# Batches 0 and 1 of a banded attention in blocks of 58 queries, v by single heads on ACT's queue, and a newly searched order

## The chip, the cores and the metric

The kernel runs on one core of one Trainium2 chip. The metric is the device time of one execution in microseconds, lower is better. The core has TensorE (PE, with its weight loads shown as PEld), VectorE (DVE), ScalarE (ACT), GpSimd (POOL) and SyncE (SP). SP, ACT and POOL also issue DMA transfers, each on a queue of its own.

## What is computed

Attention on 8 batches of 8 heads, 576 tokens, head size 64. Each head has two parts that are added: softmax attention between means of four tokens (144 pooled positions), repeated four times, and softmax attention in a band of plus or minus three tokens. Then a two-layer feed-forward with the ELU.

```python
q_d, k_d, v_d = (t.reshape(B, H, S // 4, 4, D).mean(axis=3) for t in (q, k, v))
out_up = np.repeat(sm_attn(q_d, k_d, v_d), 4, axis=2)     # softmax(q k^T / 8) v
mask = np.abs(pos[:, None] - pos[None, :]) < 4
out_local = masked_softmax(q @ k.T / 8, mask) @ v
x = (out_up + out_local).transpose(0, 2, 1, 3).reshape(4608, 512)
h = x @ w_in                                              # 512 x 2048
g = np.where(h > 0, h, np.exp(np.minimum(h, 0)) - 1)
return g @ w_out                                          # 2048 x 512
```

## The kernel before

The work is cut into named operations, each on one engine. A planner (`Plan`, a list scheduler with a rank and an assumed duration for each operation) simulates the engines while the program is built, and the operations are then written out in the order that it found. That order is fixed: each engine runs its own list in order, and waits at an operation until what it reads is there. The ranks come from the table `PARAM`, with corrections for single operations in `FIRST`. Some parameters choose the engine (`e_...`), some gate a weight load behind a cast (`G0` to `G8`, by `WGATE`) or the loads of batch 1 behind an event of batch 0 (`L0` to `L4`, by `LGATE`; a small memset on DVE holds the load back).

Heads go in pairs, j = 0 to 3 for each batch b. For a pair the operations are, by name: `load{b}{j}q` and `k` (SP, some of the k by POOL with a cast on the way), `cast{b}{j}0` and `1` to fp16, `tq` and `tk` (PE: transposes and sums of four tokens at once, L645, L648, L662), `evq` and `evk` (evictions from PSUM by ACT or DVE, L685, L686), `sc` (scores, L757), `ex` (one exponential on ACT over both parts, L787), `mask` (DVE, L792; for batch 0 the mask is instead added by PE, L763), `den` (PE sums the exponentials, L810), `recip` (DVE, L828), `spr` (PE spreads the reciprocals over the partitions, L841), `evr` (its eviction, L850), `out` (L883), `xn` (DVE normalizes, L910, L914), `add` (the pooled part is added, L933, into `xt`, blocks of 512 tokens).

v is loaded for all heads of a batch at once (`vm{b}0`, `vm{b}0h`, `vm{b}2`, `vm{b}2h`; two lots of four heads, two halves of keys), cast by `vc{b}{j}`, and pooled on PE by `tv` (L705, L722), evicted by `evv`. The local part cuts the 576 tokens into 6 blocks of 96. A block has two halves of 48 queries, each against 64 keys on 64 partitions, so that two halves and two heads fill the 128 by 128 array in four tiles of 64 by 64. Batches 0 and 1 (`SIX`) take a way of their own for q and k: their rows are loaded six tokens to a partition, in long pieces.

The feed-forward has nine blocks of 512 tokens: `mm1_{t}_{fc}` (L950, 4 matmuls of 512 columns), an exponential (ACT, L956), two operations on DVE (L958, L961), and `mm2_{t}_{tt}{part}` (L979, 4 matmuls), then `os` (ACT, L995) and the store. w_in comes in four chunks, w0 to w3 (`WI`), w_out in w4 to w7 (`WO`), all on POOL's queue, with a cast. Attention of batch b+1 is interleaved with the feed-forward of block b. Before the first mm1 there is only batch 0 and the first transposes of batch 1; where PE has nothing ready there, the planner writes matmuls on zeros (`fill`, L357).

All hardware transfers, those of SP and of ACT, share eight semaphores in turn, in the order in which the program lists them together: each transfer waits, on the engine that issues it, for the landing of the transfer eight before it.

Of the kernel before, what the change touches and what calls it, by code (L numbers as in the profile page):

```python
# [16 lines left out]
SD = S // 4  # L17
# [23 lines left out]
BY_PE = (0, 1)  # L41
WIC = (0, 512, 1024, 1536, 2048)
# [22 lines left out]
class Plan:  # L65
# [197 lines left out]
    def emit(self):  # L263
        for o in self.order:
# [8 lines left out]
PARAM = dict(e_d0=2, e_d1=0, e_d2=0, e_d3=1, M0=27.21, P=36.34, LAG=0.71, LEAD=52.25, GAP=6.32, SC=5.0,  # L273
             DEN=30.8, OUT=1.3, OUTG=2.09, LOAD=15.53, VLOAD=34.45, VCAST=9.57, warm=3.4, FILL=36.0, WI=-28.49,
             WO=59.77, WOG=5.01, OVER=1.64, LEAD1=58.97, GAP1=6.47, OUT1=55.0, VLOAD1=29.88, LOAD1=41.47,
             CC=-34.39, tv0=-22.07, C0=-2, SC0=3.1, OUTA=-23.54, OUTB=-20, DEN0=2.92, DENB=-27.58, SPA=-26.75,
             SPB=-20.86, V0=-43, G0=0, G1=0, G2=0, G3=2, G4=12, G5=6, G6=12, G7=3, G8=13, L0=0, L1=1, L2=2,
             L3=4, L4=4, LAG0=0.75, BY4=-51.82, TV1=0.68, C1=-19.87, e_cq0=0, e_cq1=1, e_cq2=1, e_cq3=1,
             e_ck0=0, e_ck1=0, e_ck2=1, e_ck3=1, e_q0=1, e_q1=0, e_q2=0, e_q3=0, e_k0=1, e_k1=1, e_k2=0,
             e_k3=0, QG=2.5, tvA=-26, e_v0=2, e_v1=1, e_v2=2, e_v3=1, e_g0=1, e_g1=1, e_g2=1, e_g3=1, e_r0=1,  # L280
             e_r1=0, e_r2=1, e_r3=1, e_xr0=0, e_xr1=1, e_xr2=0, e_xr3=1, e_a0=1, e_a1=0, e_a2=1, e_a3=0,
             e_xq0=1, e_xq1=0, e_xq2=1, e_xq3=0, e_xk0=1, e_xk1=0, e_xk2=1, e_xk3=1, KS=-64, KSG=3, e_s0=0,
             e_s1=1, e_s2=1, e_s3=0, e_xs0=0, e_xs1=1, e_xs2=1, e_w0=0, e_w1=1, e_w2=0, e_w3=0, e_xs3=0)

FIRST = {
    "add000": 0.72, "add001": 3.11, "add010": 0.8, "add011": 1.42, "add020": -0.47, "add030": 1.32,
    "add031": 0.68, "cast000": 0.77, "cast011": 1.41, "cast021": 4.15, "cast030": 0.71, "den00": -0.64,
    "den02": -0.88, "evk00": 0.17, "evk01": -0.98, "evk03": 0.21, "evq00": -5.46, "evq01": -5.01,
    "evq03": 0.38, "evr01": -3.98, "evr02": -2.25, "evv01": 6, "evv02": -2.4, "evv03": 0.21, "ex00": -5.19,
    "ex01": 5.05, "ex02": 0.83, "ex03": -1.67, "load00k": -4.99, "load01k": -2.41, "mask1": 6, "mask6": -3.11,  # L290
    "out00": -0.66, "out01": 4.25, "out02": -0.47, "out03": 1.13, "recip02": -2.47, "sc01": 0.78,
    "sc03": -0.22, "select": -0.15, "sixths": -1.87, "spr00": -2.79, "spr01": -3.25, "spr02": -1.4,
    "spr03": -1.43, "tens": 0.56, "tk00": -5.07, "tk01": -0.72, "tk02": 3.96, "tk03": 1.15, "tq00": 3.92,
    "tq01": 0.71, "tq02": -1.94, "tv00": -4.97, "vb": 1.68, "vc00": 2.37, "vc01": -3.26, "vc02": -4.17,
    "xn00": -1.03, "xn01": -5.03, "xn02": -0.06,
# [4 lines left out]
def kernel(  # L300
# [15 lines left out]
    def many(kind, shape, dt=FP16):  # L316
# [8 lines left out]
        "qt": many("qt", [128, 720]),  # L325
        "kt": many("kt", [128, S + 16]),
        "ex": many("ex", [128, 2, EW]),
        "vd": many("vd", [128, 3, NPAIR, 128]),
        "rcb": many("rcb", [128, NPAIR, 2, GW]),
        "rc": many("rc", [128, HD]),  # L330
        "xn": many("xn", [128, 2 * GW]),
# [32 lines left out]
    def const(name, shape):  # L364
        return sb.tile(shape, FP16, tag=name, name=name)
# [3 lines left out]
        "BY6": const("BY6", [QB, NB, SD]),  # L369
        "VR": const("VR", [128, 32]),  # L370
        "VB": const("VB", [128, 28]),
        "BND": const("BND", [128, KR + KB]),
        "MASK": const("MASK", [128, NB, KB]),
        "NEG": const("NEG", [128, NB, KB]),
        "FIRST": const("FIRST", [128, 32]),
        "PICK": const("PICK", [128, 2, 51]),
# [12 lines left out]
    def sixths():  # L389
        band(C["BY6"][:], [[1, NB], [-4, SD]], 6, 0, 3)  # L390

    def clears():
# [4 lines left out]
        nc.vector.memset(C["VB"][:], 0.25)  # L397
        nc.vector.memset(C["ONE"][:, QB:], 0.25)
# [5 lines left out]
    def marks():  # L404
# [5 lines left out]
        for i in range(4):  # L410
            nc.vector.memset(pick[32 * i : 32 * i + 24, 1, 19 + i // 2 : 20 + i // 2], 1.0)
        nc.vector.memset(first[:], 0.0)
# [27 lines left out]
    def mask1():  # L440
        band(C["BND"][:], [[-1, KR + KB]], 1, 0, 6)

    def mask6():
        m = C["MASK"]
        for h in range(2):
            one = C["BND"][KR * h : KR * h + KR, KR * h : KR * h + 1]
            nc.vector.tensor_copy(out=m[KR * h : KR * h + KR], in_=_free(one, [[0, NB], [1, KB]]))
        nc.vector.memset(m[0:3, 0], 0.0)

# [6 lines left out]
    def fours():  # L456
# [6 lines left out]
    c_m6 = op("DVE", 0.65, -57, mask6, after=[c_m1], name="mask6")  # L463
    c_mask = op("POOL", 0.25, -56, edge, after=[c_m6], name="edge")
    c_one = op("DVE", 0.2, PARAM["BY4"], eye_one, after=[c_eye], name="eye_one")
    c_neg = op("DVE", 0.6, -54, lambda: nc.vector.tensor_scalar(
        out=C["NEG"][:], in0=C["MASK"][:], scalar1=-1.0, scalar2=30000.0, op0=AB.add, op1=AB.mult), after=[c_mask], name="neg")
# [3 lines left out]
    c_vr = op("DVE", 0.35, -54, fours, after=[c_vb], name="fours")  # L471
# [74 lines left out]
    def load_v(b, parts=(0, 2)):  # L546
# [6 lines left out]

        def blocks(lo, hi, tok, n):
            return bass.AP(tensor=a.tensor, offset=a.offset + (lo * QB + tok) * D, ap=[[D, n], [QB * D, hi - lo], [1, D]])

        def main(c0, c1, h, eng):
            t = at(x32)[KR * h : KR * h + KR]
            if b == 0 and c0 == 0 and h == 0:
                nc.vector.memset(t[0:3, 0:1, :], 0.0)  # L560
                nc.sync.dma_start(out=t[3:KR, 0:1, :], in_=blocks(0, 1, 0, KR - 3))
                c0 = 1
# [6 lines left out]

# [526 lines left out]
```

## Time and profile before

| What | Value |
|---|---|
| Median of 3 runs | 349.24 us (347.39 to 349.95) |
| Profiled execution, its own time | 349.04 us |
| Its span, first to last instruction | 347.3 us |
| PE busy | 331.9 us, 96% |
| DVE, ACT, POOL busy | 218.0, 196.4, 132.6 us |
| Mean granted clock of TensorE | 0.984 |
| mm1 (L950), mm2 (L979) | 576 and 592 matmuls, 141.6 and 141.5 us |
| First mm1 starts at | 34.12 us |
| DMA moved | 49.73 MB, mean 143 GB/s |

Busy time of an engine overlaps that of the others. Busy times of single matmul groups overlap too, since matmuls are pipelined: 576 matmuls at a mean of 380 ns are 219 us of durations in 141.6 us of busy time. Gaps are what PE's timeline shows between groups, with what released it in brackets.

### The profile page before, as it was taken

The numbers are of one execution on the slowest core, as the hardware profiler recorded it, in microseconds if no ns is written. First come the engines' busy times: TensorE is split into PE (matmuls) and PEld (weight loads), VectorE is DVE, ScalarE is ACT, GpSimd is POOL, SyncE is SP. The second block draws the span as 40 slices with busy tenths as digits, with TensorE's granted clock in tenths as the row PEclk, the third lists the DMA queues.
The fourth block names the chain that finished last, engine by engine and source line by source line (L and its number), as shares of the span: only waits on it lengthen the run. The fifth ranks groups of instructions, "written<-read, shape, count | busy, mean of one in ns | idle before, by whom it ended". The sixth has DMA issues, their size and how long they took to land.

```text
span 347.3 us, 10965 instructions
## 1 busy us (share of the span) xinstructions
PE 331.9 (96%) x4672; PEld 172.4 (50%) x4672; DVE 218.0 (63%) x459; ACT 196.4 (57%) x337; POOL 132.6 (38%) x190
## 2 busy tenths in 40 slices
PE   6967999999999999899989999999999999999995
PEld 3744564555554455445544455545554444444443
DVE  6564788467474986377756786577657738655530
ACT  3582577297754686277817762776376325444431
POOL 6583133765449443732455246623410150000000
PEclk9896999999999999999999999999999999999999
DMA  8999999999999999999957995003100310001011
GB/s 204 208 213 243 195 191 205 176 192 233 223 186 202 237 227 224 178 244 216 192 131 141 189 202 137 32 32 87 64 32 30 90 64 30 32 30 60 32 54 67
DMA packets 120196, 49.73 MB, mean 143 GB/s; under 512 B 106996, under 2 KB 114708, under 8 KB 120148
## 3 DMA queue, kind: packets, MB, share of 16 engines
q1 hardware_dynamic: 112004, 39.33, 58.1%
q0 software_dynamic: 6592, 9.32, 14.5%
q8 instruction: 36, 0.59, 0.8%
q10 hardware_dynamic: 1552, 0.39, 0.6%
q14 instruction: 12, 0.10, 0.1%
HBM read 44.27 MB, written 9.55 MB: 155 GB/s over the span
## 4 chain that ended last, share of the span: by engine, by line
PE 58%; issue 0%; ACT 0%; DVE 0%; ACTq 0%
PE bank L979 27%; PE bank L950 24%; PE bank L662 2%; PE bank L883 2%; PE bank L757 1%; PE bank L705 1%; PE bank L810 1%; ACT os L995 0%; DVE xn L914 0%; ACTq L995 0%
## 5 line engine op out<-in xcount | busy, mean ns | idle before, releaser
L979 PE MATMUL bank<-WO,gt 128*128 128x512 f16 (+1 forms) x592 | 141.5, 374 | 1.5 <-DVE xn L914 1.2
L950 PE MATMUL bank<-xt,WI 128*128 128x512 f16 x576 | 141.6, 380 | 0.5 <-DVE gt L961 0.5
L956 ACT ACTIVATE e<-bank 128x512 f16<-128x512 f32 x144 | 86.8, 604 | 62.0 <-PE bank L950 45.1
L958 DVE TENSOR_SCALAR e<-e 128x512 f16<-128x512 f16 x144 | 58.0, 406 | 72.7 <-ACT e L956 72.5
L961 DVE SCALAR_TENSOR_TENSOR gt<-bank,e 128x512 f16<-128x512 f32 x144 | 98.6, 689 | 5.2
L979 PEld LDWEIGHTS <-gt 128*128 128x128 f16 x592 | 55.1, 98 | 60.4 <-DVE xn L914 1.7
L950 PEld LDWEIGHTS <-WI 128*128 128x128 f16 x576 | 53.5, 98 | 61.2 <-issue 2.9
L625 POOL CAST c<-ld 96x768 f16<-96x768 f32 x54 | 44.7, 839 | 34.5 <-issue 15.2
L933 POOL TENSOR_TENSOR xt<-xn 128x64 f16<-128x64 f16 (+7 forms) x62 | 40.4, 678 | 40.6 <-DVE xn L914 40.5
L995 ACT COPY os<-bank 128x512 f32<-128x512 f32 (+1 forms) x37 | 21.2, 575 | 40.9 <-PE bank L979 40.7
L910 DVE TENSOR_TENSOR xn<-bank,rcb 128x576 f16<-128x576 f32 x32 | 24.1, 753 | 22.0 <-POOL xt L933 9.8
L787 ACT ACTIVATE ex<-bank 128x1008 f16<-128x1008 f32 x32 | 31.6, 1010 | 8.3 <-PE bank L757 8.3
L572 POOL CAST v<-v 128x768 f16<-128x768 f32 x30 | 24.7, 848 | 23.1 <-DMA v<-in_v_dram 11.6
L677 ACT CAST qt<-bank 128x720 f16<-128x720 f32 x24 | 18.3, 763 | 18.6 <-PE bank L662 18.5
L662 PEld LDWEIGHTS <-c 96*128 96x128 f16 x288 | 18.9, 97 | 10.2 <-POOL c L625 0.5
L662 PE MATMUL bank<-ONE,c 96*128 96x120 f16 x288 | 22.1, 216 | 0.0
L855 POOL DMA_DIRECT2D rd<-rc x6 | 3.5, 579 | 47.2 <-DVE rc L828 44.7
L689 ACT CAST kt<-bank 128x576 f16<-128x576 f32 x24 | 15.8, 658 | 2.3 <-PE bank L662 2.3
L792 DVE TENSOR_TENSOR ex<-ex,MASK 128x576 f16<-128x576 f16 x28 | 14.9, 536 | 3.4 <-ACT ex L787 3.4
L883 PEld LDWEIGHTS <-v 64*64 64x64 f16 x768 | 9.4, 111 | 9.2 <-issue 9.1
L883 PE MATMUL bank<-ex,v 64*64 64x48 f16 x768 | 11.8, 191 | 1.8 <-issue 1.8
L757 PEld LDWEIGHTS <-kt 64*64 64x64 f16 x768 | 9.0, 109 | 8.0 <-issue 6.3
(90 smaller groups left out, 218.5 us busy)
## 6 DMA issues: line engine op xcount, KB each, us to landing
v<-in_v_dram SPq DMA_DIRECT2D x29, 384.0 KB, 7.7
ld<-in_q_dram SPq DMA_DIRECT2D x32, 288.0 KB, 6.0
out_dram<-os SPq DMA_DIRECT2D x35, 256.0 KB, 2.0
ld<-in_k_dram SPq DMA_DIRECT2D x28, 288.0 KB, 5.9
rcb<-rd POOLq DMA_DIRECT2D x12, 360.0 KB, 6.1
WI<-in_moe_w_in_dram POOLq DMA_DIRECT2D x4, 512.0 KB, 15.1
WO<-in_moe_w_out_dram POOLq DMA_DIRECT2D x4, 512.0 KB, 15.5
v<-in_v_dram SPq DMA_DIRECT2D x2, 368.0 KB, 8.5
```

The costliest lines, as they stand in the source:

```text
L572: f(out=at(x)[:, j].rearrange("p e c d -> p (e c) d"), in_=at(x32)[:, 12 * j : 12 * j + 12, :])
L625: f(out=at(y)[:], in_=at(x)[:].rearrange("p e c d -> p c e d"))
L662: nc.tensor.matmul(o, t[:, c, :, :], C["ONE"][:], start=True, stop=True)
L787: lambda: nc.scalar.activation(out=at(x)[:], in_=two(sc, 0, 128, 0, EW), func=AF.Exp, scale=SCALE),
L883: nc.tensor.matmul(PS[64 * e : 64 * e + 64, z.slot[0] + g, a : a + n], lhs, rhs, tile_position=(KR * r, 64 * e), **kw)
L910: nc.vector.tensor_tensor(out=_free(x, [[KB, 2], [QB, NB], [1, KB]]), in0=_free(zz, [[512 + HD, 2], *local]), in1=_free(yy, [[HB + SD, 2], ...
L933: f(out=at(xt(t))[:, j, o : o + n - a], in0=ln, in1=gn, op=AB.add)
L950: nc.tensor.matmul(one(h, 0, 128, 0, TBLK), WI[:, dc, 128 * fc : 128 * fc + 128], at(x)[:, dc, :], start=(dc == 0), stop=(dc == DMC - 1),)
L956: op("ACT", 0.55, r, lambda: nc.scalar.activation(out=at(e)[:], in_=one(h, 0, 128, 0, TBLK), func=AF.Exp), reads=[h], writes=[e], name=f"e ...
L958: op("DVE", 0.42, r, lambda: nc.vector.tensor_scalar(out=at(e)[:], in0=at(e)[:], scalar1=1.0, scalar2=-1.0, op0=AB.min, op1=AB.add), reads ...
L961: op("DVE", 0.64, r, lambda: nc.vector.scalar_tensor_tensor(out=at(gt)[:, fc, :], in0=one(h, 0, 128, 0, TBLK), scalar=0.0, op0=AB.max, in1 ...
L979: nc.tensor.matmul(one(z, 0, 128, cols.start, cols.stop), at(gt)[:, fc, 128 * tt : 128 * tt + 128], WO[:, fc, cols], start=(fc == 0), stop ...
```

## The change

It concerns batches 0 and 1 in the attention, and the order of everything.

- The local part of batches 0 and 1 takes 5 blocks of 116 tokens (two halves of 58 queries, each against 64 keys) instead of 6 of 96: 20 matmuls of 58 columns for 24 of 48 in scores and outputs of a pair. In the scores the last block has 60 columns, which fill up rows of 4 x 73 sums.
- Their pooled sums are made with `U = 73` columns a group instead of 72, so that `ex` has 1022 elements for 1008 and `rcb` 730 for 720.
- Masks and pooling constants of their own: `MASM`, `VC`, `VM`, larger `NEG` and `PICK`; `MASK` and `VR`, now needed from batch 2 on, are made later.
- v of batches 0 and 1 is loaded by single heads, 4 transfers of 5 blocks where 1 transfer had 24 (one more for the first edge), and cast in pieces of 640 elements instead of 768.
- `PARAM` and `FIRST` are new throughout.

```diff
+MB, MP, MU = 58, 116, 73
+MW = 4 * MU
+MX = 5 * MP
...
-PARAM = dict(e_d0=2, ..., M0=27.21, P=36.34, LAG=0.71, ..., FILL=36.0, ...
-             G0=0, G1=0, G2=0, G3=2, G4=12, G5=6, G6=12, G7=3, G8=13, L0=0, L1=1, L2=2, L3=4, L4=4,
-             ... e_q0=1, e_q1=0, e_q2=0, e_q3=0, e_k0=1, e_k1=1, e_k2=0, e_k3=0, ...
-             ... e_s0=0, e_s1=1, e_s2=1, e_s3=0, ... e_w0=0, e_w1=1, e_w2=0, e_w3=0, ...)
+PARAM = dict(e_d0=1, ..., M0=36.0, P=34.14, LAG=0.89, ..., FILL=18.57, ...
+             G0=2, G1=1, G2=8, G3=5, G4=12, G5=12, G6=13, G7=13, G8=13, L0=1, L1=2, L2=2, L3=9, L4=3,
+             ... e_q0=0, e_q1=0, e_q2=1, e_q3=1, e_k0=1, e_k1=1, e_k2=1, e_k3=0, ...
+             ... e_s0=0, e_s1=0, e_s2=1, e_s3=1, ... e_w0=1, e_w1=1, e_w2=1, e_w3=1, ...)
...
+        def main_m(i, h, eng):
+
+            t = at(x32)[KR * h : KR * h + KR]
+            for e in range(2 * i, 2 * i + 4):
+                c0 = 0
+                if b == 0 and e == 0 and h == 0:
+                    nc.vector.memset(t[0:3, 0:1, :], 0.0)
+                    eng.dma_start(out=t[3:KR, 0:1, :], in_=bass.AP(
+                        tensor=a.tensor, offset=a.offset, ap=[[D, KR - 3], [MP * D, 1], [1, D]]))
+                    c0 = 1
+                eng.dma_start(out=t[:, 5 * e + c0 : 5 * e + 5, :], in_=bass.AP(
+                    tensor=a.tensor, offset=a.offset + (e * S + MB * h - 3 + MP * c0) * D,
+                    ap=[[D, KR], [MP * D, 5 - c0], [1, D]]))
...
-                op(by(i, h), 0.45, r + 0.1 * i + 0.01 * h,
...
+                op(by(i, h), 1.6 if m else 0.45, r + 0.1 * i + 0.01 * h,
...
-                op(eng, {"DVE": 0.55, "POOL": 0.85, "ACT": 0.8}[eng],
+                op(eng, {"DVE": 0.48, "POOL": 0.73, "ACT": 0.7}[eng] if m else 0.85,
...
-                        turn(c, z.slot[0] + 1, HB, SD, C["BY6"][:, c], start=(c == 0), stop=(c == NB - 1))
+                        turn(c, z.slot[0] + 1, HB, SD + 1, C["BY6"][:, c], start=(c == 0), stop=(c == NB - 1))
...
-            for i in range(NB):
+            for i in range(5) if m else ():
+                n = MB if i < 4 else MB + 2
+                for h, e, p in tiles:
+                    t = MP * i + MB * h
+                    put(e, h, MB * i, n, kt[p, t : t + KR], qt[p, t : t + n], start=not hide, stop=not hide or i == 4)
+            for i in () if m else range(NB):
...
-                for i, u in enumerate(HD * k for k in range(7)):
-                    rr, kind = NR * e + min(i, 4), i // 4
+                for i, u in enumerate(U * k for k in range(7)):
+                    rr, kind = NR * e + min(i, 4), i // 4 if b not in SIX else (0, 0, 0, 0, 2, 2, 3)[i]
...
-            for i in range(NB):
+            m = b in SIX
+            n, w, u = (MB, MW, MU) if m else (KB, HB, HD)
+            for i in range(5 if m else NB):
                 for h in range(2):
                     for e in range(2):
-                        put(h, e, h, HD * h + KB * i, KB, v_[half[h], j, e, i, :],
-                            ex[half[h], e, KB * i : KB * i + KB], start=True, stop=True)
+                        put(h, e, h, u * h + n * i, n, v_[half[h], j, e, i, :], ex[half[h], e, n * i : n * i + n],
+                            start=True, stop=True)
```

What the planner makes of it, as the lists of the engines begin (names only):

```text
ACT before: vm00h select evq00 evk00 ex00 evk01 ex01 vc00 ex02 evv00 evv01 ex03 vc02 evr00 cast100 evv02 cast101 evr02 evv03 evr03 evq10 ...
ACT after:  vm00 vm00h vm02 select vm02h evk00 evq02 evk01 ex00 ex01 evk02 evq03 ex02 evv03 ex03 evr01 evr03 evr02 evq10 evq11 exp0_0 ...
SP before:  load00k load00q load01q load02q load03q load03k vm00 vm02 vm02h load10q load10k load11q load13q ...
SP after:   load00k load00q load01q load01k load02q load03q load10q load10k load11q load12q load13q load13k vm10 vm10h vm12 vm12h ...
PE before:  fill x10, tq00 tk00, fill x3, tq01 sc00 tk01 tq02 tk02 sc01 tq03 tk03 sc02 den00 tv00 sc03 spr01 spr00 out01 den02,
            fill x2, tv02 out00 spr02 spr03, fill x4, out02 out03, fill x3, tq10, fill, tk10, fill, mm1_0_0 sc10 tq11 ...
PE after:   fill x16, tk00, fill x6, tq00, fill x7, tq02 tq01, fill x4, tk01, fill x5, sc00 sc01 tk03 tk02 tq03 den00 tv02
            sc02 sc03 tv00 spr00 den02 out00 spr01 spr03 out01 out02 spr02 out03 tq10 tk10 tq11 mm1_0_0 mm1_0_1 sc10 ...
DVE after, ahead of mm1: ... recip00 evv02 (gates of load10, vm10) evv00 evr00 (gates of load11, load12) evv01 recip02
            xn00 add000 xn01 xn02 xn03 cast110 add030 ...
POOL before: load01k load02k ... vc01 w0 w1 load11k w2 vc03 w3 load12k add011 w7 add000 add001 w5 ... vc10 vc11 w4 w6 vc12 vc13
POOL after:  load02k load03k ... vc01 w1 vc03 vc02 w0 load11k load12k cast100 add001 cast101 w3 ... w2 ... vc10 vc11 w4 w5 vc12 vc13 cast200 w6 w7
```

PE has 4618 matmuls after (38 of them fills) for 4672 (28 fills).

## The prediction

> **What bounds the kernel now.** First the page (busy time), then busy time by stretch.
>
> ```profile
> PE 331.9 (96%) x4672; PEld 172.4 (50%) x4672; DVE 218.0 (63%) x459; ACT 196.4 (57%) x337; POOL 132.6 (38%) x190
> ```
> ```profile
> 20.00:25.00 5.00, 3.07 (x127) 2.16 (x128) 3.79 (x11) 4.07 (x6) 4.11 (x7) 1.00 1.14 206
> 25.00:30.00 5.00, 1.92 (x5) 0.44 (x4) 0.56 (x1) 1.15 (x3) 1.65 (x3) 0.56 1.19 245
> 30.00:35.00 5.00, 5.00 (x106) 3.26 (x105) 3.21 (x6) 1.64 (x4) 2.95 (x4) 0.76 1.19 232
> ...
> 300.00:305.00 5.00, 5.00 (x25) 2.28 (x24) 2.82 (x7) 2.11 (x4) 0.00 (x0) 1.00 0.00 0
> ```
>
> PE is the bound once the first product with w_in (mm1, L950) has started: from there to the end its waits sum to only some 4 us (0.52, 0.39, 1.20, 1.12, 0.30 and 0.28 in PE's timeline). So the time is the start of mm1 plus a nearly fixed amount of PE work. I call that start T1. It is the last line of the next fence, from the timeline of the head:
>
> ```profile
> 0.81 0.74 ACTq L568 DMA_DIRECT2D v<-in_v_dram  x1
> ...
> 1.58 1.28 ACT L438 ACT_TABLE_LOAD   x1 [1.58 <-PEq L1080]
> ...
> 5.86 1.26 ACT L438 COPY SEL<-TEN 128x1280 f16<-128x1280 f16 x1 [3.00 <-DVE TEN L431]
> ...
> 6.53 0.56 DVE L625 CAST c<-ld 96x768 f16<-96x768 f32 x1 [0.71 <-DMA ld<-in_q_dram]
> ...
> 8.95 0.82 POOL L625 CAST c<-ld 96x768 f16<-96x768 f32 x1 [1.80 <-DMA ld<-in_q_dram]
> ...
> 10.73 0.82 POOL L625 CAST c<-ld 96x768 f16<-96x768 f32 x1 [0.78 <-DMA ld<-in_q_dram]
> ...
> 12.26 1.01 ACT L787 ACTIVATE ex<-bank 128x1008 f16<-128x1008 f32 x1 [2.73 <-PE bank L757]
> ...
> 18.94 1.02 ACT L787 ACTIVATE ex<-bank 128x1008 f16<-128x1008 f32 x1
> ...
> 34.12 1.03 PE L950 MATMUL bank<-xt,WI 128*128 128x512 f16 x4
> ```
>
> Three casts wait for transfers of q that land at 6.5, 8.9 and 10.7: the second, third and fourth load on SP's queue. ACT runs the four exponentials of batch 0 between 12.3 and 20.0, and T1 follows 14.2 us later. Part of that is a gap on PE:
>
> ```profile
> 20.00 0.34 PE L883 MATMUL bank<-ex,v 64*64 64x48 f16 x18 [0.31 <-issue]
> ...
> 28.08 0.21 PE L841 MATMUL bank<-rc,SEL 32*128 32x72 f16 x1 [4.47 <-issue]
> ...
> 176.02 0.24 PE L883 MATMUL bank<-ex,v 64*64 64x48 f16 x6 [1.12 <-issue]
> ```
> ```profile
> q8 instruction: 1, 0.02, 12.3%
> ```
>
> The first three lines are PE's timeline, the fourth the DMA view of 25.0 to 25.5. "Issue" is a wait with no releaser: the gap falls between the 19th and the 20th matmul of one spread (L841). Counting PE's instructions in the built order (a weight load and a matmul each count one), the gaps at 20.0 and 28.1 lie 256 apart, and so do, in multiples of 256, those at 106.7, 176.0 and 211.2. One packet of the instruction queue shows a few us after each such crossing. I read it as PE waiting for its next 256 instructions. From one crossing to the resumption at the next, where PE had to wait: 16.9 to 20.0 (3.2 us, no weights moving), 20.0 to 28.1 (8.1 us, weights and k on POOL's queue), later 6.5 to 9.2 us.
>
> **The change, part by part.**
>
> PE work. Scores and outputs of a pair of heads go from 24 local matmuls of 48 columns to 20 of 58 (60 in the last scores block). 288 columns become 290, and 72 matmuls of the steady form take 0.73 us (61.58 to 62.31), 10 ns each for 48 columns: streaming gives nothing, instruction count at most 8 matmuls x 4 pairs x 10 ns = 0.3 us in batch 1. I take -0.15. Batch 0 lies before T1, where PE waits anyway.
>
> Bytes of v. 40 blocks instead of 48 in two batches: 5,120 packets instead of 6,144. From 12 to 16 us the queue moved 2,784 of these packets in 4 us, so a batch's v is some 1.4 us shorter, and each cast has 640 columns for 768. These help the head only if v sets it.
>
> Constants. Longer memsets on DVE and one more band on POOL, about 1 us each, before the first casts. They lie beside the loads that land at 6.5 and later; uncovered they would cost that 1 us.
>
> ACT's queue, where I see the price. All of batch 0's v is now issued by ACT, head by head: 13 transfers ahead of the table load and `select`, four behind `select`, and then `evk00`, ACT's first eviction. Before it was one. In the built program each transfer from SP or ACT waits on its engine for the one eight earlier on the two together, and two of ACT's waits are for SP's loads: the thirteenth for q of pair 2, the fifteenth for q of pair 3. SP's load of q2 in turn waits for q0 (6.5) and is fifth on SP's queue instead of fourth, with v moving beside it: after 10.7, near the fifth's cast at 11.7 plus the sharing, so 12.5. ACT then: an issue 0.5 (SP's four took 2.17), table load 1.28, `select` 1.26, four issues 2.2: 17.8 (16 if q2 lands with 10.7, 18.8 with 0.74 an issue). Its first eviction in the profile began at 7.99. Queued behind it: all ACT evictions, so `sc00`, `sc01` on PE, and everything after.
>
> From there, with E = 17.8. Three evictions of 0.85 and two exponentials of 1.0: E+4.55. `evk02`, `evq03` (1.7, 0.4 of waiting for transposes): E+6.6. `tv02` stands ahead of `sc02` on PE and needs the v whose four transfers left at E: they land after 2 to 5.5 us, two casts 0.73 each, so E+4 to E+7. With `sc02` 0.65, ex02, an eviction of 0.37 and ex03, ACT ends the fourth exponential at E+10.4 = 28.2 (E+9.3 to E+10.7), against 20.0.
>
> Then `den02` 0.6, reciprocal 0.7, `spr03` 0.35, `out01` and `out02` 1.0, `spr02` 0.35, `evr02` 0.75 with handoffs of 0.1: 32.5. DVE: `xn02`, `xn03` 1.05 each, `cast110` 0.6, `add030` 0.75: T1 = 36.1. The other arm ends at the same time: batch 1's first loads are now gated behind `recip00` (some 24.4) instead of free, land after some 7 us (7.0 and 6.6 for those issued at 16.8 to 17.6), and POOL has cast100, cast101, a weight issue and two adds of 0.87 behind them.
>
> The instruction blocks. By the same count the multiples of 256 now fall in the last fill before `sc00`, in `tq03`, in `spr00`, in `out02` and in `sc10`. `tq03` runs at 22.9, `spr00` is due at 26, `out02` at 31. The trace prices a block at 3.2 to 8.1 us; here POOL's queue carries two weight chunks and two loads of k rather than six and two, so below the middle, 5.0. First crossing: 22.9+5.0 = 27.9, covered, since `den02` waits for the exponential until 28.2. Second: 27.9+5.0 = 32.9 against 31, 1.9 us. T1 = 38.0 (36.1 at 3.2 us with 0.6 more at most; near 44 at 8.1).
>
> A page of the Trainium skill speaks against that term: Runtime: NRT & Kernel Launch, section "Instruction fetch mechanics", says that blocks of 256 instructions are fetched while the current one runs and the crossing is mostly hidden. By it the 1.9 us would go; the gap of 4.47 us in this trace doesn't agree in a dense stretch.
>
> After T1. `tq11` now stands ahead of T1 (12 matmuls, -0.65), the smaller scores -0.15, the four fills that stood behind T1 took 1.2 us and covered waits, of which I give half, -0.6: -1.4. Later blocks: crossings pair up in out20/out22, out30/out32 and out40/out42, 6.5 to 7.2 us apart, against 6.5 to 9.2 for a block: 0 to 2 us each, where before 1.8 us went in three gaps. I take +1.0 more (-1.8 to +4). All four chunks of w_out are now issued after the casts of batch 1's v, two of them were at 23.4 and 25.9: the last would land within a us or two of `mm2_0_03`; +0.5 (0 to 4).
>
> Sum against the profiled execution (span 347.3, time 349.04, beside a median of 349.24): 349.04 + (38.0 - 34.1) - 1.4 + 1.0 + 0.5 = 353.0.
>
> **The rivals.**
>
> The blocks stay hidden. Only ACT's late start counts: T1 36.1, no later term: 349.04 + 2.0 - 1.4 = 349.6, and up to 351 with w_out. For it: many crossings in the profile show no gap. Against: the head is denser in instructions than anything that crossed freely. (The skill's rule above would give this.)
>
> Faster. ACT's transfers run beside SP's without delaying them and ACT is free at 14: T1 = 14 + 18.3 = 32.3, the 4.47 us gap does not come back, and 349.04 - 1.8 - 1.4 = 345.8; if also the other waits behind T1 shrink, 344. It decides from E below 15.8, where T1 equals the old one. For it: from 4 to 8 us three queues together moved 263 GB/s, with v alone 180. Against: q2 must then land at 9, and as the fourth load it came at 10.7.
>
> Weights late. With SP sending batch 2 beside w_out, its chunks take what two of WI took (16.8 and 18.1 us) instead of 7.7 and 9.0: PE waits up to 4 us in the first mm2: 357. For it: all four chunks are bunched. Against: POOL's queue is empty before them.
>
> **Chances.** The forecast (ACT late and blocks) 0.40, blocks hidden 0.25, faster 0.23, weights late 0.12. An outcome within 1% (3.5 us, about what a measurement here can tell from no change) is nearly all of the second and edges of the others; faster by over 1% most of the third with little from elsewhere. Slower 0.51, within 0.27, faster 0.22. Range: 346.0 (E near 14) to 358.0 (weights late, or a block of near 8 us); the forecast's own range, from E 16 and 3.2 us a block to E 18.8 and 6.5, is 349 to 356.
>
> **What would show it.** Right: `evk00` on ACT at 17 or later, behind v transfers whose waits show on ACT's queue; the fourth exponential ending after 27; PE gaps by "issue" in `spr00` or `out02`; mm1 starting at 36 to 41; after that PE over 97% busy. Wrong: ACT's first eviction before 15, or mm1 before 34; then the time is below 349. If T1 is right and the time is not, the waits sit in the first mm2 (w_out) or in the out phases.

## The result and the profile after

The changed kernel takes 362.32 us (median of 6 runs, 361.92 to 364.44) against 349.96 us for the kernel before (median of 6): ratio 1.0383, 95% interval 1.0342 to 1.0424. It is slower, as forecast, but by 12.4 us and not by 4, and it lies above the range. The profiled execution took 362.46 us, with a span of 360.7 us (before 347.3) and a mean granted clock of 0.966 (before 0.984). Of two of the experiments below, e2 and e8, the profile is of a disturbed execution, so from these only the order of events is read, and of e8's times only 360.3 us counts.

The busy line of the page after:

```profile
PE 340.2 (94%) x4618; PEld 177.8 (49%) x4618; DVE 214.3 (59%) x476; ACT 195.0 (54%) x335; POOL 134.5 (37%) x197
```

54 matmuls fewer, and 8.3 us more busy time on PE: the work has shrunk and runs slower. Busy time by stretch after (busy time and instructions of PE, PEld, DVE, ACT, POOL; then granted clock, DMA share, GB/s) tells where:

```profile
15.00:20.00 5.00, 1.80 (x19) 1.80 (x19) 0.00 (x0) 3.26 (x5) 1.14 (x2) 0.50 0.43 91
...
35.00:40.00 5.00, 4.26 (x89) 3.71 (x88) 5.00 (x9) 1.59 (x3) 4.20 (x6) 0.55 1.11 200
40.00:45.00 5.00, 5.00 (x48) 2.52 (x52) 2.31 (x5) 1.68 (x4) 2.66 (x5) 0.50 0.33 48
...
65.00:70.00 5.00, 1.96 (x14) 0.60 (x14) 1.21 (x3) 1.44 (x3) 2.32 (x4) 0.62 1.17 218
```

Three slumps: one before T1 (the start of the first mm1), one across it, one at 65 us. Before, PE worked from 35 us on at a clock of 1.00; the same stretches of the kernel before, as far as they lie behind its T1:

```profile
35.00:40.00 5.00, 5.00 (x121) 3.08 (x121) 3.68 (x10) 2.86 (x5) 0.96 (x2) 1.00 1.23 196
40.00:45.00 5.00, 5.00 (x66) 2.53 (x63) 4.20 (x10) 3.04 (x5) 0.00 (x0) 1.00 1.24 207
...
65.00:70.00 5.00, 5.00 (x107) 3.18 (x107) 1.85 (x4) 2.49 (x5) 4.98 (x9) 1.00 1.09 183
```

The timeline after, ACT's issues, POOL, ACT and PE together in order of time (start, duration, then what ended the idle time before it):

```profile
1.36 13.10 ACTq L622 DMA_DIRECT2D v<-in_v_dram  x12
...
13.99 0.82 POOL L685 CAST c<-ld 96x768 f16<-96x768 f32 x1 [2.89 <-DMA ld<-in_q_dram]
...
14.50 1.28 ACT L451 ACT_TABLE_LOAD   x1 [14.50 <-DMA v<-in_v_dram]
...
17.32 0.64 ACT L745 CAST kt<-bank 128x576 f16<-128x576 f32 x1 [0.27 <-issue]
...
18.20 0.28 PE L705 MATMUL bank<-BY,c 96*128 96x145 f16 x1 [7.33 <-ACT kd L746]
...
30.38 1.04 ACT L858 ACTIVATE ex<-bank 128x1022 f16<-128x1022 f32 x1
...
34.95 0.26 PE L959 MATMUL bank<-ex,v 64*64 64x58 f16 x9 [0.41 <-issue]
...
41.09 3.61 PE L1030 MATMUL bank<-xt,WI 128*128 128x512 f16 x8
...
68.04 1.44 PE L771 MATMUL bank<-v,VM 128*32 128x512 f16 x9 [3.51 <-POOL v L629]
...
69.44 4.54 PE L1030 MATMUL bank<-xt,WI 128*128 128x512 f16 x12
...
236.16 2.75 PE L1030 MATMUL bank<-xt,WI 128*128 128x512 f16 x12 [0.48 <-DVE gt L1041]
```

ACT is held by its v transfers until 14.5 (before: free at 1.6), its first eviction comes at 17.32, and PE stands still for 7.33 us until that eviction frees a pair of PSUM banks. T1 is 41.09 (before 34.12): 7.0 of the 13.4 us. The other 6.4 lie behind T1: 3.51 us at `tv1`, which waits for batch 1's v; then the slow clock: the first 8 matmuls of mm1 take 3.61 us where 8 take 1.89 at full clock, and the 12 behind `tv1` take 4.54 us where 12 take 2.75, together 3.5 us.

### The profile page after: what moved, and what is told of

Same layout as the page of the kernel before. It is cut to its first block, busy times and chain, and to the rows that moved or that the text cites. A ratio compares the mean times of both kernels' runs of the same rounds, so it can differ in the third digit from the quotient of the medians.

```text
span 360.7 us, 10912 instructions
## 1 busy us (share of the span) xinstructions
PE 340.2 (94%) x4618; PEld 177.8 (49%) x4618; DVE 214.3 (59%) x476; ACT 195.0 (54%) x335; POOL 134.5 (37%) x197
## 3 DMA queue, kind: packets, MB, share of 16 engines
q10 hardware_dynamic: 5374, 1.31, 2.0%
## 4 chain that ended last, share of the span: by engine, by line
PE 75%; DMA 13%; DVE 4%; SPq 3%; issue 2%; ACT 2%; ACTq 1%; POOL 0%; DVEq 0%; POOLq 0%
PE bank L1059 31%; PE bank L1030 29%; DMA rcb<-rd 5%; DMA v<-in_v_dram 5%; PE bank L722 4%; SPq L622 3%; PE bank L959 2%; PE bank L823 2%; DMA ld<-in_q_dram 2%; PE bank L705 1%; PE bank L771 1%; DMA rd<-rc 1%; PE bank L886 1%; DVE e L1038 1%; DVE xn L990 1%
## 5 line engine op out<-in xcount | busy, mean ns | idle before, releaser
L1038 DVE TENSOR_SCALAR e<-e 128x512 f16<-128x512 f16 x144 | 55.9, 391 | 75.6 <-ACT e L1036 74.9
L685 POOL CAST c<-ld 96x768 f16<-96x768 f32 x57 | 46.8, 833 | 28.8 <-DMA ld<-in_q_dram 12.8
L990 DVE TENSOR_TENSOR xn<-bank,rcb 128x576 f16<-128x576 f32 (+1 forms) x32 | 24.1, 753 | 27.4 <-PE bank L959 17.5
L858 ACT ACTIVATE ex<-bank 128x1008 f16<-128x1008 f32 (+1 forms) x32 | 31.5, 1016 | 3.3 <-PE bank L823 3.1
L722 PEld LDWEIGHTS <-c 96*128 96x128 f16 x288 | 18.8, 97 | 12.2 <-issue 3.1
L631 POOL CAST v<-v 128x768 f16<-128x768 f32 x24 | 19.6, 836 | 4.1 <-DMA v<-in_v_dram 4.1
L705 PE MATMUL bank<-BY,c 96*128 96x145 f16 x72 | 10.5, 266 | 8.3 <-ACT kd L746 7.3
L705 PEld LDWEIGHTS <-c 96*128 96x128 f16 x144 | 11.2, 116 | 11.1 <-POOL c L685 4.8
L808 ACT CAST vd<-bank 128x512 f16<-128x512 f32 x21 | 11.7, 588 | 5.1 <-PE bank L771 5.1
```

Source lines behind the costliest of these rows:

```text
L685: f(out=at(y)[:], in_=at(x)[:].rearrange("p e c d -> p c e d"))
L705: nc.tensor.matmul(PS[:, bank, a : a + n], t[:, c, :, :], con, **kw)
L722: nc.tensor.matmul(o, t[:, c, :, :], C["ONE"][:], start=True, stop=True)
L858: lambda: nc.scalar.activation(out=at(x)[:, :, 0:w], in_=two(sc, 0, 128, 0, w), func=AF.Exp, scale=SCALE),
L990: nc.vector.tensor_tensor(out=_free(x, [[n, 2], [2 * n, c], [1, n]]), in0=_free(zz, [[512 + u, 2], *local]), in1=_free(yy, [[k + 2 * u, 2] ...
L1038: op("DVE", 0.42, r, lambda: nc.vector.tensor_scalar(out=at(e)[:], in0=at(e)[:], scalar1=1.0, scalar2=-1.0, op0=AB.min, op1=AB.add), reads ...
```

## The experiments

In every run the two numbers to watch are T1 and what follows it, span minus T1. T1 and span are from one profiled execution of each kernel; the ratio is that of the times of all its runs, so the two need not agree to the microsecond (the profiled executions of e10, e13 and e14 were the fastest of theirs).

| Kernel | T1 | span - T1 | ratio to before (95%) |
|---|---|---|---|
| before | 34.12 | 313.2 | |
| changed | 41.09 | 319.6 | 1.0383 (1.0342 to 1.0424) |
| e15: blocks in the order of before, large v lots | 34.31 | 313.2 | 1.0037 (1.0001 to 1.0073) |
| e6: single heads in the kernel before | 42.14 | 312.8 | 1.0188 (1.0140 to 1.0236) |
| e17: blocks and single heads, order of before | 40.10 | 316.3 | 1.0284 (1.0249 to 1.0318) |
| e12: changed, large v lots by ACT | 38.83 | 317.8 | 1.0165 (1.0050 to 1.0280) |
| e13: changed, large v lots by SP | 39.13 | 316.6 | 1.0346 (1.0253 to 1.0440) |
| e18: as e13, v behind batch 0's q | 35.83 | 318.0 | 1.0161 (1.0120 to 1.0203) |
| e14: changed, three places mended | 36.79 | 315.6 | 1.0225 (1.0135 to 1.0314) |
| e10: changed, boundaries moved | 44.95 | 325.6 | 1.0714 (1.0601 to 1.0827) |

**First theory: ACT's hold alone.** The v transfers of batch 0 issued by SP, each at its old place in the order.

```diff
-  ... main_m(i, h, nc.scalar if by(i, h) == "ACT" else nc.sync) ...
+  ... main_m(i, h, nc.sync) ...
```

> The changed kernel with every operation in its planned order; only the 17 transfers of batch 0's v are issued by SP instead of ACT, at their places in the program. Theory (ACT's late start is the cause): the first eviction of k on ACT starts near 7.5 us instead of 17.3, the fourth exponential ends near 24 instead of 31.4, the first mm1 starts near 34 instead of 41.1, and less clock is lost behind it: 350 us (347 to 354). Rival 1 (the searched order is bad by itself, whoever issues v): the first mm1 stays past 39 and the time above 358. Rival 2 (PE's 3.5 us wait for batch 1's v and the clock behind it are a cause of their own): 354 to 356, with that wait still there.

361.79 us, ratio 1.0348 (1.0273 to 1.0423). ACT was free, and yet T1 was 40.86. From ACT's and PE's timelines of this run:

```profile
8.26 0.64 ACT L745 CAST kt<-bank 128x576 f16<-128x576 f32 x1 [0.89 <-PE bank L705]
```
```profile
14.76 0.24 PE L705 MATMUL bank<-BY,c 96*128 96x145 f16 x1 [3.08 <-POOL c L685]
...
26.27 0.49 PE L788 MATMUL bank<-v,VM 128*32 128x256 f16 x9 [3.34 <-POOL v L629]
```

The first eviction is 9 us earlier. PE then waits at `tq02` for a cast of batch 0's own q, and at `tv02`, which stands ahead of `sc02` in its list, for v. The theory fell: where ACT's hold ends, the late q and v take over.

**Blocks or order?** e2: the new blocks with `PARAM` and `FIRST` of before. e3: the new `PARAM` and `FIRST` on the old blocks.

> The new blocks of 58, v by single heads, with the parameters and rank corrections of the kernel before (planned anew with them; one of the four lots of v on ACT, four transfers). Theory: the blocks themselves cost little, ACT is held for some 2 us of issues; within -1 to +3 us of before: 351. Rival (the blocks, or 17 small transfers, carry the loss): 356 to 362.

> The kernel before, blocks of 48 and v in four large transfers, with the new parameters and rank corrections (planned anew). ACT issues all four lots of v, and the third and fourth wait for two loads of SP, ahead of the table load. Theory: ACT comes free near 11 to 12 us, between the two kernels, first mm1 at 36 to 38: 353 to 357. Rival (the order is bad whatever ACT waits for): 360 and more. If the order is good once ACT is not held long: 347 to 350.

e2: ratio 1.0449 (1.0347 to 1.0551); e3: 394.19 us, 1.1304 (1.1228 to 1.1379). Neither divides the loss. In e2 the planner, with its price of 1.6 for a v operation in place of 0.45, had put batch 1's first cast ahead of the last exponential on ACT, which then waited for q. In e3 the new ranks work on shapes and durations for which they were not searched; whether that is the reason was not tested. Ranks and shapes are one object here; the division came from e15 and e17, which keep the planner's price as well.

**The wait at `tv1`.** In the changed order, the two gates and loads of batch 1's last pair, with v behind them on SP, are moved up behind `xn03`.

```diff
+    o13 = [o for o in plan.order if o.name in ("gload13q", "gload13k", "load13q", "load13k")]
+    plan.order = [o for o in plan.order if o not in o13]
+    at13 = 1 + max(i for i, o in enumerate(plan.order) if o.name in ("xn03", "cast101"))
+    plan.order[at13:at13] = o13
```

> The changed kernel, with only the gates and loads of q and k of batch 1's last pair placed behind xn03 instead of behind the first ELU, so that v of batch 1, queued behind them on SP, leaves some 6 us earlier. Theory: PE's wait of 3.5 us before tv1 goes, and with it the slow clock behind (70 to 75 us at 0.69), the head stays (first mm1 at 41): 357.5 (356 to 359). Rival (v would be late anyway, w_out being issued beside it): the wait stays over 2 us, 361 or more.

358.89 us, 1.0278 (1.0197 to 1.0359): about 3.5 us gained. The time lies at the upper end of what was expected: span minus T1 fell from 319.6 to 315.0, but T1 came later, at 42.61. The wait at `tv1` is gone and another shows that it had covered, for w_out in the first mm2:

```profile
74.07 1.89 PE L1059 MATMUL bank<-WO,gt 128*128 128x512 f16 x8 [2.05 <-DMA WO<-in_moe_w_out_dram]
```

**Number of transfers.** e5 fetches v in 10 transfers of 8 heads (one block of 64 tokens each, 128 KB) instead of 16, 11 for batch 0, all at the place of the first lot. e6 does the reverse in the kernel before: each v transfer of 24 blocks of batches 0 and 1 is cut into four, nothing else. e8 also lets ACT issue all of batch 0's.

```diff
...
+            while c0 < c1:
+                c2 = c0 // NB * NB + NB
+                eng.dma_start(out=t[:, c0:c2, :], in_=blocks(c0, c2, KB * h - 3, KR))
+                c0 = c2
```

> The changed kernel with its order, engines and blocks as they are; only v of batches 0 and 1 is fetched otherwise: for each half of the tokens five transfers, one for each block, of 64 tokens by 8 heads (131 KB), in place of eight by single heads (82 KB): 11 for batch 0 and 10 for batch 1 instead of 17 and 16. Theory (the number of transfers holds ACT, and v with it): ACT is held until some 8 to 11 us instead of 14.5, the first eviction ends its wait by 12 to 14 instead of 17.3, the first mm1 starts at 37.5 to 39.5 instead of 41.1, batch 1's v is issued in 7 to 10 us instead of 12.0 and the wait at tv1 falls from 3.5 to under 1.5 us; 353 to 358 us. Rival (the rate is that of rows of 256 bytes beside the weights, not of the number of transfers): v lands when it did, the first mm1 after 40.5, tv1 as before, 360 to 363.

> The kernel before with its blocks and its order as they are; only each v transfer of 24 blocks of batches 0 and 1 is cut into four of 6 blocks (98 KB), on the same engines: 17 and 16 transfers instead of 5 and 4. Theory (single heads alone cost much of the change): SP is busy with batch 0's v to about 16 to 20 us, batch 1's q and k and the casts behind them come 4 us or more later, the first mm1 starts at 36 to 39 instead of 34.1; 352 to 357 us. Rival (the cut costs nothing that is not hidden; blocks and order did it): the first mm1 within 0.7 us of 34.1, 348.5 to 350.5.

> The same cut in the kernel before, and all of batch 0's v transfers issued by ACT ahead of its table load, as in the changed kernel; blocks and order are those of before. Theory (ACT held by its transfers delays the head): the table load ends at 14 to 16 us, the first eviction on ACT waits for it, the first mm1 starts at 38 to 42, 354 to 360 us. Rival (ACT's hold is no loss, since SP is free for batch 1's q and k and v comes at the same time): no later than the same cut on SP, 349 to 353.

e5: 361.31 us, 1.0324 (1.0265 to 1.0383). ACT was held longer, to 17.1, and T1 came at 43.65. The theory in this form is wrong: fewer transfers that step over the heads are no quicker (all of batch 0's v was issued by 17.1, in the changed kernel by 17.3). e6: 356.62 us. The cut alone, in an order that had not been touched, costs 6.6 us, all of it before T1 (42.14), none behind (312.8). From the timelines, SP's issues before, then e6's: SP's issues, POOL's cast, PE's wait for it, and ACT's next wait:

```profile
7.55 6.92 SPq L568 DMA_DIRECT2D v<-in_v_dram  x3
```
```profile
10.45 10.15 SPq L573 DMA_DIRECT2D v<-in_v_dram  x12
```
```profile
31.25 0.82 POOL L578 CAST v<-v 128x768 f16<-128x768 f32 x1 [7.05 <-DMA v<-in_v_dram]
```
```profile
32.11 0.83 PE L728 MATMUL bank<-v,VR 128*32 128x256 f16 x12 [6.04 <-POOL v L578]
```
```profile
33.03 0.83 ACT L631 CAST c<-ld 96x768 f16<-96x768 f32 x1 [5.10 <-DMA ld<-in_q_dram]
```

Twelve transfers occupy SP for 10.15 us (before: three for 6.92), so v is late and batch 1's q, queued behind it, is late too. And while they run the transfer engines are only about half as busy as before. Busy time by stretch of the kernel before, then of e6, 10 to 20 us:

```profile
10.00:15.00 5.00, 5.00 (x144) 4.05 (x146) 2.46 (x6) 1.72 (x3) 2.46 (x3) 0.81 1.31 201
15.00:20.00 5.00, 4.69 (x192) 3.71 (x178) 3.77 (x11) 4.41 (x6) 3.40 (x5) 1.00 1.16 210
```
```profile
10.00:15.00 5.00, 4.78 (x92) 3.98 (x94) 1.34 (x4) 1.83 (x3) 2.03 (x5) 0.59 0.64 143
15.00:20.00 5.00, 5.00 (x88) 4.21 (x84) 2.78 (x6) 1.73 (x2) 3.08 (x4) 0.50 0.66 141
```

The last two columns: a share of 1.31 and 1.16 at 201 and 210 GB/s before, 0.64 and 0.66 at 143 and 141 GB/s with the cut. e8: 360.3 us; in its profile ACT's table load comes behind all 17 transfers, and PE waits for ACT's first eviction. That ACT's issuing adds to the cut is likely there, its size is open.

**What the single heads cost in the changed kernel.** The blocks of 58 by 64 don't follow each other at one distance across heads, so the true data can't be fetched in large lots. e12 fetches wrong tokens in lots of 20 blocks, with all shapes and work kept; e13 issues these by SP.

```diff
...
+            eng.dma_start(out=t[:, 5 * e + c0 : 5 * e + 20, :], in_=bass.AP(
+                tensor=a.tensor, offset=a.offset + (e * S + MB * h - 3 + MP * c0) * D,
+                ap=[[D, KR], [MP * D, 20 - c0], [1, D]]))
```

> The changed kernel with its blocks, order and engines; v of batches 0 and 1 is fetched in lots of 20 blocks (64 tokens by 1280 numbers, 328 KB) as if the blocks of four heads followed each other at one distance, 5 and 4 transfers instead of 17 and 16. They don't, so from the second head of a lot on the tokens are wrong ones; all the work and its shapes stay. It tells what the single heads cost in the changed kernel, which the true data do not allow to take away. Theory (the single heads are most of the loss): ACT is free by 4 to 7 us, its first eviction comes by 10, PE's wait of 7.3 us ahead of tq02 falls under 2, the first mm1 starts at 34 to 37 instead of 41.1, no wait at tv1; 349 to 354 us. Rival (the new order, with its late gates and its place of tv02, is slow by itself): the first mm1 after 38, 356 or more.

> As the run with v in large lots (wrong tokens from a lot's second head on, all shapes and work kept), and batch 0's lots issued by SP instead of ACT. Theory (what is left of the loss is ACT held by DMA issues): table load at 1 us, ACT's first eviction at 7 to 9, no long wait of TensorE in the head, the first mm1 at 33 to 36, 349 to 353 us. Rival (the order is late by itself: gates of batch 1's loads, tv02 ahead of sc02): the first mm1 at 37 or later, 355 to 358.

e12: 357.73 us; e13: 360.88 us (its profiled execution was its fastest, 357.41). The wait at `tv1` is gone in both, and T1 came down by 2 us only. Both rivals hold: on the ratios 5.8 us (1.7 to 9.8) are left in e12 and 12.1 (8.9 to 15.4) in e13 that are neither single heads nor, since e13 is no faster than e12, ACT's issuing. e13 shows what stands behind it, in ACT's, POOL's and PE's timelines:

```profile
7.46 0.64 ACT L744 CAST kt<-bank 128x576 f16<-128x576 f32 x1
```
```profile
14.54 1.70 POOL L684 CAST c<-ld 96x768 f16<-96x768 f32 x2 [2.23 <-DMA ld<-in_q_dram]
```
```profile
15.42 0.30 PE L704 MATMUL bank<-BY,c 96*128 96x145 f16 x1 [4.55 <-POOL c L684]
```

ACT evicts at 7.46, and PE waits for a cast of batch 0's own q, which landed behind v. In the changed kernel the row of POOL at 13.99 is the same wait, hidden behind ACT's hold. e18 moves the v lots behind the last of batch 0's loads on SP.

```diff
+    vm = [o for o in plan.order if o.name in ("vm00", "vm00h", "vm02", "vm02h")]
+    plan.order = [o for o in plan.order if o not in vm]
+    at_ = 1 + next(i for i, o in enumerate(plan.order) if o.name == "load03q")
+    plan.order[at_:at_] = vm
```

> As the run of the new order with v in large lots by SP (wrong tokens from a lot's second head on), and the first two v transfers, which stood ahead of three of batch 0's k and q loads on SP, moved behind them all. Theory (v ahead of q is what holds the new order's head): POOL's casts of q start by 10 to 12 instead of 14.5 us, TensorE's wait of 4.6 us ahead of tq02 falls under 2, the first mm1 at 36 to 37.5 instead of 39.1; 1.5 to 3 us less than that run. Rival (a later wait takes its place, tv02 for v above all): the first mm1 at 38.5 or later, the same time.

354.80 us, 6 us less than e13 by the medians, but only 1.8 by the two profiled executions (T1 3.3 earlier, 1.4 more behind it); PE's timeline:

```profile
13.56 0.24 PE L704 MATMUL bank<-BY,c 96*128 96x145 f16 x1 [1.66 <-POOL c L684]
...
35.83 2.89 PE L1029 MATMUL bank<-xt,WI 128*128 128x512 f16 x8
...
73.02 1.36 PE L721 MATMUL bank<-ONE,c 96*128 96x120 f16 x12 [4.25 <-DVE xn L993]
```

The wait fell from 4.55 to 1.66 and T1 by 3.3 us: v ahead of q holds the head of the new order, shown. The 4.25 us behind it, for batch 2's first transposes, stand in e12 and e13 as well (4.32 and 3.76).

**Blocks alone, and blocks with single heads, in the order of before.** Both keep `PARAM`, `FIRST` and the planner's price of before; they differ in the v transfers.

> The blocks of 58 by 64 with the parameters of the kernel before (so nearly its order), v of batches 0 and 1 in lots of 20 blocks at one distance (wrong tokens from a lot's second head on, all shapes and work kept). Theory (the blocks are harmless, only the single heads and the new order cost): first mm1 at 33 to 36, 346 to 350 us, if the boundaries of 256 instructions fall as well as before. Rival (the blocks themselves cost, or their shifted boundaries do): 352 or more, and then either gaps ended by nothing shown of 5 us or more in sum (boundaries), or none and longer work (blocks).

> The blocks of 58 by 64 with the parameters of the kernel before and with the planner's price of a v operation left at 0.45 (so nearly the order of before), v by single heads, on the true data; the run with large lots differs from it in the v transfers alone. Theory (blocks cost nothing, single heads about 7 us, in the order of before too): 356 to 360 us, the first mm1 at 38 to 41; so the new order adds 2 to 6 us more. Rival (the new order repays a part of what the single heads cost): 363 to 368.

e15: 351.04 us, T1 34.31, and 313.2 behind it, the very figure of before: the blocks bring nothing, and cost 1.3 us (0.03 to 2.6). e17: 358.72 us, T1 40.10. ACT's and PE's timelines of e17:

```profile
26.97 0.73 ACT L628 CAST v<-v 128x640 f16<-128x640 f32 x1 [8.30 <-DMA v<-in_v_dram]
```
```profile
28.67 0.24 PE L885 MATMUL bank<-ex,FIRST 128*32 128x73 f16 x2 [8.12 <-ACT ex L857]
```

ACT waits 8.30 us for v with the last exponential queued behind that cast. So the loss divides, on ratios times 349.5 us: blocks 1.3, single heads 8.6 (1.0284 less 1.0037), new order 3.5 (1.0383 less 1.0284), in sum 13.4. The last two are each uncertain by some 1.8 us. Taken the other way round, with the order ahead of the single heads, the runs give 4.5 for the order (e12 less e15) and 7.6 for the single heads (changed less e12), each uncertain by some 4 us: the two ways agree within the noise. Between the two orders the blocks of 256 instructions (below) also fall at other places, which no run here holds fixed.

**The clock.** e7 puts dummy matmuls on zeros where PE waited; e9 does it with numbers (256 and 256 instructions) that shift no later boundary of 256.

```diff
+    for name, n, own in (("tq02", 33, False), ("den02", 2, True), ("tq10", 1, True), ("mm1_0_0", 1, True), ("tv1", 16, True)):
+        warm(name, n, own)
```
```diff
+    idle("tq02", 128, 128, False)
+    idle("tv1", 128, 64, True)
```

The arguments are the operation that the matmuls stand ahead of, their number and, in `idle`, their columns (512 in `warm`).

> The changed kernel with dummy matmuls of zeros added on TensorE where it waited: 33 ahead of tq02 (7.3 us of idle), 2 ahead of den02, one each ahead of tq10 and the first mm1, 16 ahead of tv1 (3.5 us); nothing else is changed. Theory (the lost granted clock behind idle stretches is paid by the work that follows): the clock stays near 1.00 from 15 to 22 and from 66 to 75 and, if the gaps between 30 and 36 caused it, from 36 to 46 as well; the mm1 of the first 4.5 us takes half as long, the span is 2 to 5 us shorter, 356 to 360 us. Rival (the clock falls there for another reason, the many small matmuls say, or the chain of other engines sets those stretches anyway): within 1 us of 362.

> The changed kernel with dummy matmuls that shift no block of 256 instructions: 128 of 128 columns (256 instructions, some 7 us) ahead of tq02 and 128 of 64 columns (256 more, some 4 us) ahead of tv1, where TensorE waited 7.3 and 3.5 us. Theory (the slow clock behind the two waits costs time): clock near 1.00 from 15 to 22 and from 66 to 75, the first mm1 0.3 to 1 us earlier, the mm1 behind tv1 1.5 us shorter, 358 to 360.5 us. Rival (the clock behind these waits is covered by other waits): 361 to 363.

e7: 369.54 us, 1.0574 (1.0517 to 1.0632); e9: 363.89 us, 1.0389 (1.0313 to 1.0464), no different from the changed kernel. The clock stayed at 1.00 from 15 to 30 in both and from 65 to 75 (before the fills: 0.50 and 0.62), but across T1 it fell in both, in e7 to 0.59 and 0.73, in e9 to 0.50 all the same. Busy time by stretch of e9, then a row of its PE timeline, where what it gained behind `tv1` went into the next wait:

```profile
35.00:40.00 5.00, 4.40 (x106) 3.92 (x96) 4.96 (x9) 2.23 (x4) 4.20 (x6) 0.50 1.01 182
40.00:45.00 5.00, 4.65 (x25) 2.50 (x23) 2.63 (x6) 1.43 (x3) 3.57 (x6) 0.50 0.46 68
```
```profile
79.10 1.89 PE L1059 MATMUL bank<-WO,gt 128*128 128x512 f16 x8 [1.62 <-DMA WO<-in_moe_w_out_dram]
```

The two long waits are not what slows the clock across T1, and a faster clock behind `tv1` brought nothing here, since w_out came when it did. e9 is not a clean test of the time, though: it has two gaps by issue of its own, 1.26 us at 31.6 and 1.02 at 67.0, against 0.41 in the changed kernel, and its T1 is 42.00. Why the clock falls at 35.5 in the changed kernel stays open; from 30 to 36 PE has small matmuls and no gap longer than 0.48 us.

**Where the boundaries fall.** e7 was slower by 7 us, and its PE timeline shows why it can't be read as a test of the clock:

```profile
191.96 2.71 PE L1059 MATMUL bank<-WO,gt 128*128 128x512 f16 x8 [2.74 <-issue]
...
229.66 0.30 PE L959 MATMUL bank<-ex,vd 64*64 64x72 f16 x12 [2.74 <-issue]
```

Two gaps ended by nothing shown, far behind the added matmuls. e10, e16 and, for the kernel before, e11 add only small matmuls (32 columns) inside an existing wait:

```diff
+    idle("tq02", 64, 32, False)
```
```diff
+    idle("tq02", 32, 32, False)
```
```diff
+    idle("tq00", 50, 32, False)
```

That is 128 instructions in e10, 64 in e16 and 100 in e11.

> The changed kernel with 64 dummy matmuls of 32 columns (128 instructions, some 2 us) ahead of tq02, inside its wait of 7.3 us: they cost no time of their own and move every later boundary of 256 instructions on TensorE half a block. Theory (where the boundaries fall is worth microseconds: with 106 instructions added two gaps of 2.74 us appeared at 192 and 230 us): gaps ended by nothing that the profile shows add up to 2 to 7 us, against 0.4 in the changed kernel, 363 to 369 us. Rival (the boundaries cost nothing much; the earlier loss came from the dummy matmuls ahead of tv1): gaps under 1 us, 361 to 362.5.

> The changed kernel with 32 dummy matmuls of 32 columns (64 instructions, some 1 us) ahead of tq02, inside its wait of 7.3 us; every later boundary of 256 instructions on TensorE comes a quarter of a block earlier in the work. Theory (the boundaries' places decide): gaps ended by nothing shown at other places than in the changed kernel, 1 to 7 us in sum, 362 to 370 us. Rival (the 14 us of the half block's shift were an accident of other waits): 361 to 363, gaps under 1 us.

> The kernel before with 50 dummy matmuls of 32 columns (100 instructions, some 1.4 us) ahead of tq00, inside TensorE's wait of 1.65 us: the boundary of 256 instructions that stood in spr03 (gap 4.47 us) comes 100 instructions earlier in the work, in den02, and so do all later ones. Theory (the place of the boundaries decides what they cost): the sum of such gaps changes by 2 us or more from 6.3, in either direction, and the time with it: 345 to 348, or 351 to 354. Rival (TensorE would wait there for batch 1's casts anyway): within 1 us of 349.5.

e10: 376.29 us, 14 us more than the changed kernel, from 2 us of matmuls that PE had time for. Its PE timeline:

```profile
41.48 0.24 PE L705 MATMUL bank<-EYE,c 96*128 96x96 f16 x1 [2.08 <-issue]
...
191.34 0.26 PE L959 MATMUL bank<-ex,vd 64*64 64x72 f16 x7 [2.74 <-issue]
...
229.89 0.36 PE L959 MATMUL bank<-ex,v 64*64 64x48 f16 x11 [2.59 <-issue]
```

Gaps by issue of 0.35 us and more sum to 8.7 us (0.81, 0.47, 2.08, 2.74, 2.59) against 0.41 in the changed kernel. They are 8.3 of the 9.8 us by which the span of this execution, the fastest of its four, is longer; the granted clock was 0.72 from 190 to 195 us and 0.68 from 230 to 235. What makes the others slower still stays open. e16: 363.12 us, 1.0398 (1.0318 to 1.0478), gaps of 0.50 and 1.70, no loss that can be told from noise. e11: 350.59 us, 1.0045 (1.0003 to 1.0088): the gap of 4.47 at 28.1 became 2.65 at 17.3 and 1.93 at 33.8, T1 37.34, but 311.6 behind it. So the place of the boundaries is worth from nothing to 14 us in this program, and the changed order stands well in this.

**Mending three places, on the true data.** ACT issues only the first lot's 9 transfers, the gates of e4 move up, and `tv02` with its eviction goes behind `sc03`.

> The changed kernel, true data: of batch 0's v only the lots of the first four heads are issued by ACT (9 transfers), the others by SP; batch 1's last gates and loads stand behind xn03; tv02 and its eviction on DVE stand behind sc03. Theory (each of the three waits found is real and they add): ACT's first eviction at 9 to 12 us, the first mm1 at 37 to 39, no wait at tv1, 353 to 357 us. Rival (the v transfers' rate decides, whoever issues them): the first mm1 at 40 or later, 357 to 360.

358.36 us (354.11 to 359.15). T1 36.79 in its fastest execution, the profiled one, no wait at `tv1`: the three waits are real, but by the median it gains no more than e4 alone. No version on true data came near the kernel before.

## Why the prediction was right or wrong, point by point

- **Direction, and the start of the chain: right.** ACT's first eviction was put at 17.8 and came at 17.32. The trace agrees with thirteen transfers ahead of the table load and two pairs behind it. That the number is so near is in part luck: the table load, due at 13.0 by the sum, came at 14.50, because q of pair 2 landed near 14.0 and not at 12.5, and the four issues counted as 2.2 us ran beside the table load and `select` and cost 0.27.
- **E to the fourth exponential: the step that failed in the head.** It was put at 10.4 and took 14.1 (17.32 to 31.42). The sum had ACT's evictions and exponentials follow each other; the profile has PE standing until 18.20, since `tq02` needs the banks that this very eviction frees, so all transposes of the second half came after E and not beside ACT's wait, with PE at half clock until 21.9. I had followed what waits for ACT's results and not what waits for the banks that it frees.
- **From there to T1: right in sum by luck, by other terms.** 9.8 was said (7.9 and 1.9 for a block), 9.7 measured. The crossing in `out02` stood where it was forecast and took some 4.7 us (from the start of `spr00` at 30.29 to 34.95, said 5.0), but PE had been late as well, so it cost 0.41 and not 1.9; the slow clock and an add on DVE (2.12 us for 0.7) took the rest.
- **Later blocks +1.0, w_out +0.5: neither came.** No gap by issue behind T1, no wait for w_out. Both prices are real (e10; e4 and e9), they were hidden or not met at these places.
- **Missing terms: batch 1's v, and the clock.** 16 transfers on SP instead of 4 were seen only as fewer bytes, 1.4 us for the good, and left out of the sum; their rate was never asked. They ended at a wait of 3.51 us, which e4 took away. The clock has no sentence and no price in the prediction: 3.61 for 1.89 and 4.54 for 2.75 us are 3.5 us. With T1 3.1 later than said, 3.5, 3.5, and without the 1.5 that did not come, 353.0 becomes 361.6, against 362.46.
- **The cause was put in the wrong place.** The prediction charged ACT's queue and its order. The runs charge the cut of v first (6.6 to 8.6 us, whoever issues it), the order second (3.5), ACT's issuing by itself, in the changed kernel, nothing that was measured (e1, e13). The bytes of v stood in the sum with nothing and in the argument as a help, while the cut of v was the largest cost.
- **Rivals.** "Blocks stay hidden" was right on the gaps and wrong on the time. "Weights late" named a wait that is there, one place further back. "Faster" rested on ACT free at 14 and an undelayed q: ACT was free at 14.5, and q was delayed, with the fifth load's cast at 13.99 instead of 12.5.
- The Trainium skill (Runtime: NRT & Kernel Launch, "Instruction fetch mechanics") says that crossing a block of 256 instructions is mostly hidden. The changed kernel agrees, with 0.41 us in all; the same program with 128 instructions more doesn't, with 8.7 us.

## What to carry to other kernels

Cutting a transfer changes its rate and the time that its queue is held, not only its count: before changing a tile so that its rows no longer run on at one distance, cut the old transfers and time that. For a wait that goes or comes, ask also which buffers its instruction frees, and which load of another queue would be the last to arrive if it were gone. In a program that is written out straight, put shifts of some dozens to a hundred instructions beside any comparison of orders: here 128 alone moved the time by 14 us, and 64 by nothing that could be told from noise.

## What the runs showed of the hardware that was not expected

- v in pieces of 96 KB moved at 141 to 143 GB/s with the transfer engines at a share of about 0.65, where pieces of 384 KB beside other loads had 201 to 210. Ten pieces of 128 KB over eight heads (e5) were no quicker: 143 GB/s from 15 to 20 us, at a share of 0.91. Whether size, number in flight or the pattern sets it was not separated.
- Half a block's shift (e10) made gaps of 2.74 and 2.59 us at 191 and 230 us, both among the small matmuls of the local output (L959); 53 matmuls more (e7) made gaps of 2.74 us at nearly the same two times. Between its two gaps the trace of e10 counts 512 matmuls and 512 weight loads, four times 256 instructions.
- In the changed kernel the granted clock went from 1.00 to 0.50 at 35.5 us, after a stretch in which PE was busy 3.8 of 5 us, and back to 1.00 at 45.8, 4.7 us into mm1. The Trainium skill (TensorE: Matmul & The Clock Gate, "Part 1: The HAM clock gate (the "warmup" mystery)") has the clock restored after about 3.4 us of sustained work; the trace is near that with 3.7 us at 18.2 to 21.9, and longer with 4.7 us here. A fall without a long wait is not what I had expected.
